# An attention and feed-forward kernel: the first k and q loads cast by GpSimd, and four later loads moved between queues

## The chip, the cores and the metric

The kernel runs on one core of one Trainium2 chip. The core has five engines that run their own instruction streams and wait for each other through semaphores: TensorE (PE: matrix products and transposes, its weight loads shown as PEld), VectorE (DVE), ScalarE (ACT), GpSimd (POOL) and SyncE (SP, which only issues DMAs here). DMAs are issued by SyncE and by GpSimd; the profile shows SyncE's as the hardware queue q1 and GpSimd's as the software queue q0, and both run on the same 16 DMA engines. The metric is device time in microseconds; less is better.

## The reference

Attention over 8 batches of 8 heads, 576 positions and 64 channels, with a causal mask and a bias that grows with the summed positive part of `s`; then a gated feed-forward block on the 4608 rows.

```python
scale = 1.0 / np.sqrt(D)
scores = scale * np.matmul(q, k.transpose(0, 1, 3, 2))
s_pos = np.maximum(s, 0.0)
cum = np.cumsum(s_pos, axis=-1)
bias = -(cum[:, :, :, None] - cum[:, :, None, :])
scores = np.where(causal, -1000000000.0, scores + np.minimum(bias, 0.0))
scores = scores - np.max(scores, axis=-1, keepdims=True)
attn = np.exp(scores)
attn = attn / (np.sum(attn, axis=-1, keepdims=True) + 1e-09)
return np.matmul(attn, v).astype(np.float32)
...
x = np.ascontiguousarray(attn_out.transpose(0, 2, 1, 3)).reshape(B * S, H * D)
...
g = x @ w_gate
silu = g * (1.0 / (1.0 + np.exp(-g)))
val = x @ w_val
return (silu * val @ w_out).astype(np.float32)
```

The inputs are float32; the kernel's products take bfloat16.

## The kernel before

The 64 heads are worked in 16 groups of four (`hb`, called batches of k and q here). For a group, k and q come in as float32 tiles `rawk`, `rawq` (`load_one`, L141), are cast to the bfloat16 tiles `ck`, `cq`, transposed, and put into the `KQ` tiles of pair `hb % 2`. Groups 0 to 4 are transposed by TensorE (`pe_transpose`, L295; `pe_transpose_half`, L306, for group 0) and copied out of the PSUM banks by `pe_out` (L319); groups 5 to 15 are written to a scratch in DRAM (`scratch`, L272) and read back with a transposing DMA (`transposes`, L281), then copied by `split` (L286). The 64 other rows of each `KQ` half carry the bias: `aug` (L183) copies rows of `HL`, which holds the summed `s` as high and low parts, into them. For the very first head the kernel does not wait for that DMA: `pick` (L910) multiplies the `HL` rows by a selecting matrix and `picked_row` (L920) writes the result.

`score_piece` (L352) makes a quarter of one head's scores (L373), ScalarE's exponential (L383) writes them to `pt`, and from head 8 on GpSimd cuts the causal triangle (L388, L393). For the first eight heads a product with `lower` (L367) does that. `av_piece` (L400) multiplies `pt` with the V tiles `VT` (L410; a column of ones gives the sums), `av_out` (L418) divides. V comes in five chunks per batch (`load_v`, L156) and is cast by `cast_v` (L167). The rows become `XT` by transposes on TensorE (`x_pe`) or by DMA.

The feed-forward block takes tiles of 512 rows: `gate_value` (L658) has 12 steps of a gate product (L643), a tanh on ScalarE (L664), a product on VectorE (L666), a value product (L643) and another product on VectorE (L677); `down_plain` (L692, tiles 0 and 1) multiplies by the output weight (L700), `down_seven` (L727) does the same in seven products per pair of halves. Weights are loaded and cast on the way by GpSimd's DMAs (`w_load`, L335): `WG`, `WV` in two column halves, `WO` in two row halves.

The order on every engine is the order of the program text (`tc.manual_schedule()`). From L949 the opening is written out by hand, heads 0 to 7 whole. Then the loop at L1059 walks the feed-forward items of each row tile; `n` counts them (a gate or a value step counts 1), and `at_item(n, f, ...)` (L1051) puts a call behind the item at which the count reaches n. Between the items, `pump` pulls attention steps of the later heads; `side` (L481) puts loads, casts and scratch steps at fixed steps of these. GpSimd casts V 1's chunks in `side` at head 11, last piece, and head 12. Group 5's k and q are cast by GpSimd at head 15 and go through the scratch.

A DMA that reuses a semaphore first waits for the earlier DMA on it: GpSimd's and SyncE's DMAs each take eight semaphores in turn. Tiles of a tag with `bufs=3`, such as `rawk` and `rawq`, are three in turn; `rawv` is one tile, so V 1 is not loaded before V 0 has been cast.

## Time and profile before

| | us |
|---|---|
| median of 3 runs | 374.07 |
| lowest, highest | 373.37, 374.59 |
| the profiled execution | 373.92 |
| its span, first to last instruction | 372.0 |

The granted TensorE clock of the span is 0.998. By stage, from a table of windows (busy us of each engine; the DMA column is the mean busy share of the 16 DMA engines, which can pass 1 where packets overlap):

| stage, us | PE | DVE | ACT | POOL | DMA |
|---|---|---|---|---|---|
| 0 to 5 | 3.56 | 3.77 | 4.02 | 4.03 | 0.55 |
| 5 to 10 | 4.11 | 4.86 | 3.92 | 4.95 | 0.91 |
| 10 to 15 | 4.31 | 4.91 | 4.27 | 4.94 | 0.98 |
| 15 to 19 | 3.45 | 3.94 | 4.00 | 3.94 | 1.06 |
| 19 to 24 | 5.00 | 3.65 | 4.62 | 4.53 | 1.05 |
| 24 to 29 | 5.00 | 3.41 | 2.97 | 4.07 | 1.27 |
| 29 to 35 | 5.22 | 5.67 | 4.99 | 1.15 | 1.23 |
| 35 to 55 | 19.85 | 15.76 | 15.05 | 11.48 | 1.20 |
| 55 to 85 | 29.75 | 18.75 | 22.30 | 20.17 | 0.93 |
| 85 to 365 | 279.60 | 223.21 | 172.96 | 153.14 | 0.61 |
| 365 to 372 | 3.34 | 3.14 | 0.82 | 0.00 | 0.42 |

Matmuls are pipelined and their ends modelled, so that a TensorE busy by this table is not TensorE at its peak. GpSimd's time includes the issuing of its DMAs, shown as DMA_DIRECT2D instructions with a duration. In the lines of a timeline or of a chain the first two columns are the start and the duration in us.

### The profile page before, as it was taken

The page shows a single profiled execution, that of the slowest core. Times are in us where ns is not written, and L with a number is a line of the kernel's source. Part 1 is how long each engine was busy: PE and PEld are TensorE (multiplying, and loading weights), DVE is VectorE, ACT ScalarE, POOL GpSimd, SP SyncE. Part 2 cuts the span into 40 slices and gives each one's busy share as a digit, 9 for nine tenths or more (in the row PEclk, how much of TensorE's full clock was granted, in tenths as well). Part 3 has the DMA queues.
Part 4 walks back from the last instruction along what each step waited for, and adds up shares of the span by engine and source line. Part 5 has one row for each costly group of instructions (what it writes and reads, how often), then busy time and mean ns, then how long its engine had stood idle before and what let it go on. Part 6 is the DMA issues. An engine that isn't in the chain of part 4 may idle for free.

```text
span 372.0 us, 8786 instructions
## 1 busy us (share of the span) xinstructions
PE 363.2 (98%) x3288; PEld 230.3 (62%) x3288; DVE 291.1 (78%) x585; ACT 239.9 (65%) x470; POOL 212.4 (57%) x325
## 2 busy tenths in 40 slices
PE   7899999999999999999999999999999999999996
PEld 6684556655555557855685558655865585476465
DVE  8978776377985899589967897699868867975984
ACT  8877776778886967688757875786565523323321
POOL 8983556955266547594749464955675516315320
PEclk9999999999999999999999999999999999999999
DMA  7999999799879996996789484994142113002003
GB/s 238 220 254 259 215 272 257 239 299 227 252 172 307 199 268 181 162 285 217 214 179 263 160 185 157 265 210 114 40 121 62 35 30 118 0 3 86 28 0 113
DMA packets 97133, 64.21 MB, mean 173 GB/s; under 512 B 77228, under 2 KB 82724, under 8 KB 97092
## 3 DMA queue, kind: packets, MB, share of 16 engines
q1 hardware_dynamic: 84964, 41.46, 46.9%
q0 software_dynamic: 12128, 22.21, 22.7%
q8 instruction: 25, 0.41, 0.5%
q14 instruction: 16, 0.13, 0.1%
HBM read 37.90 MB, written 19.86 MB: 155 GB/s over the span
## 4 chain that ended last, share of the span: by engine, by line
PE 83%; DVE 10%; DMA 2%; ACT 2%; issue 2%; POOL 1%; DVEq 0%; ACTq 0%
PE banks L643 43%; PE banks L749 17%; PE banks L373 9%; PE banks L410 7%; PE banks L700 5%; DVE kq L330 3%; DMA pk<-ks 2%; DVE pp L666 2%; DVE ht L677 1%; DVE kq L288 1%; ACT th L664 1%; POOL vt L173 1%; ACT pt L383 1%; PE banks L459 1%; PE banks L301 0%
## 5 line engine op out<-in xcount | busy, mean ns | idle before, releaser
L383 ACT ACTIVATE pt<-banks 128x512 bf16<-128x512 f32 (+1 forms) x256 | 120.4, 511 | 29.8 <-PE banks L373 17.1
L643 PE MATMUL banks<-XT,wg 128*128 128x512 bf16 x432 | 111.4, 379 | 0.4 <-DVE pp L666 0.3
L643 PE MATMUL banks<-XT,wv 128*128 128x512 bf16 x432 | 110.9, 379 | 0.1
L664 ACT ACTIVATE th<-banks 128x512 bf16<-128x512 f32 x108 | 64.7, 599 | 56.3 <-PE banks L643 51.4
L666 DVE SCALAR_TENSOR_TENSOR pp<-th,banks 128x512 bf16<-128x512 bf16 x108 | 73.7, 682 | 18.3 <-ACT th L664 18.0
L677 DVE SCALAR_TENSOR_TENSOR ht<-pp,banks 128x512 bf16<-128x512 bf16 x108 | 74.1, 687 | 10.3
L373 PE MATMUL banks<-kq 128*128 128x128 bf16 (+4 forms) x576 | 76.4, 240 | 0.8 <-DVE kq L330 0.3
L686 POOL TENSOR_TENSOR ht<-ht 128x512 bf16<-128x512 bf16 x35 | 40.4, 1154 | 53.3 <-DVE su L684 53.2
L373 PEld LDWEIGHTS <-kq 128*128 128x128 bf16 x576 | 46.1, 98 | 30.7 <-issue 2.4
L643 PEld LDWEIGHTS <-wv 128*128 128x128 bf16 x432 | 38.4, 98 | 36.2 <-issue 0.2
L643 PEld LDWEIGHTS <-wg 128*128 128x128 bf16 x432 | 38.4, 98 | 34.1 <-issue 0.7
L410 PEld LDWEIGHTS <-pt 128*128 128x128 bf16 x960 | 41.8, 98 | 17.7 <-issue 0.7
L388 POOL TENSOR_SCALAR_AFFINE_SELECT pt<-pt 128x512 bf16<-128x512 bf16 x56 | 36.6, 653 | 25.9 <-ACT pt L383 21.7
L410 PE MATMUL banks<-vt,pt 128*128 128x65 bf16 x960 | 46.8, 194 | 0.5 <-DVE ot L427 0.4
L444 POOL DMA_DIRECT2D xs<-ot x24 | 21.7, 904 | 30.4 <-DVE ot L427 28.0
L749 PEld LDWEIGHTS <-ht 128*128 128x128 bf16 x336 | 31.2, 98 | 4.3
L427 DVE TENSOR_TENSOR ot<-banks,rc 128x320 bf16<-128x320 f32 x64 | 31.5, 492 | 2.2
L188 POOL DMA_DIRECT2D kq<-HL x48 | 29.2, 610 | 0.0
L700 PE MATMUL banks<-wo,ht 128*128 128x512 bf16 x96 | 25.8, 379 | 0.0
L749 PEld LDWEIGHTS <-su 128*128 128x128 bf16 x252 | 23.6, 98 | 3.3
L814 POOL TENSOR_TENSOR ysb<-ysb 128x512 f32<-128x512 f32 x12 | 15.2, 1269 | 15.3 <-DVE ysb L808 15.3
L749 PE MATMUL banks<-WS,ht 128*128 128x256 bf16 x168 | 22.9, 273 | 0.0
(101 smaller groups left out, 377.2 us busy)
## 6 DMA issues: line engine op xcount, KB each, us to landing
out_dram<-ysb POOLq DMA_DIRECT2D x32, 256.0 KB, 4.0
rawv<-in_v_dram SPq DMA_DIRECT2D x28, 256.0 KB
rawk<-in_k_dram SPq DMA_DIRECT2D x12, 576.0 KB
rawq<-in_q_dram SPq DMA_DIRECT2D x12, 576.0 KB
xs<-ot POOLq DMA_DIRECT2D x24, 160.0 KB, 3.7
ks<-ck SPq DMA_DIRECT2D x11, 288.0 KB
qs<-cq SPq DMA_DIRECT2D x11, 288.0 KB
rawk<-in_k_dram POOLq DMA_DIRECT2D x3, 576.0 KB, 6.0
```

What stands on the lines that cost most here:

```text
L373: nc.tensor.matmul(sc[:, o : o + w], T[:, 1, e * S + 128 * tj : e * S + 128 * (tj + 1)], T[:, 0, e * S + lo : e * S + hi], start=not maske ...
L383: nc.scalar.activation(pt[:, c0 : c0 + n], sc, AF.Exp, scale=0.125)
L388: nc.gpsimd.affine_select(pt[:, 1088:1600], pt[:, 1088:1600], pattern=[[0, 4], [1, 128]], compare_op=ALU.is_ge, fill=zreg, base=0, channel ...
L410: nc.tensor.matmul(av[:, bi * (D + 1) : (bi + 1) * (D + 1)], pt[:, c0 : c0 + 128], VT[b % 2][:, tj, h, :], start=(tj == 0), stop=(tj == bi),)
L427: nc.vector.tensor_mul(ot[:, :, e * D : (e + 1) * D], av3[:, :, 0:D], rc[:, :, None].to_broadcast([128, NCH, D]),)
L643: nc.tensor.matmul(view(bs, TT), w[:, c, f0 : f0 + 128], xt[:, c, :], start=(c == 0), stop=(c == 3),)
L664: nc.scalar.activation(th, pg, AF.Tanh, scale=0.5)
L666: nc.vector.scalar_tensor_tensor(pp, in0=th, scalar=1.0, in1=pg, op0=ALU.add, op1=ALU.mult)
L677: nc.vector.scalar_tensor_tensor(hp[:, 2 * k2 : 2 * k2 + 2, :].rearrange("p a n -> p (a n)"), in0=pp, scalar=0.5, in1=pv, op0=ALU.mult, op ...
L686: (nc.vector if ft == NFT - 1 else nc.gpsimd).tensor_sub(hp[:, 1:3, :], hp[:, 1:4:2, :], hp[:, 0:3:2, :])
L700: nc.tensor.matmul(view(pys[ts_], DM), hps[ft // 2][:, 2 * (ft % 2) + half, c0 : c0 + 128], WO[j][:, ft % WKO, :], start=(ft == 0), stop=( ...
L749: nc.tensor.matmul(ps, lhs(p), rhs(p), start=(first and p == 0), stop=(last and p == NP - 1), skip_group_check=True,)
```

## The change

Six parts:

- k and q of group 0 (heads 0 to 3) are loaded by GpSimd in four half loads (`load_first`) that cast to bfloat16 on the way, into a tile ordered by pair of heads (`firsts`), instead of by SyncE in float32. The two casts on ScalarE and the two on GpSimd (`cast_half`) go. GpSimd's order at the start becomes: k and q of the first pair of heads, `ident`, k and q of the second pair, k and q of group 1, then the other memsets. The four copies of the first pair's k and q out of PSUM are all on ScalarE (the last was on VectorE).
- TensorE's warming products take a tile of zeros, `idle`, instead of `ident`, 31 instead of 32. `pick` runs the two low-part and the two high-part products of both sides in turn. The memset of `aug_rows(0, 0)` stands earlier on VectorE.
- The pad memsets cover only the k side, and those of the second pair of tiles stand behind `init_vt(0)`.
- V 0's loads on GpSimd stand ahead of group 1's q cast but for the fifth chunk, which stands behind it.
- V 1 is issued by GpSimd, a chunk each at items 5, 6, 7, 8 and 11, instead of by SyncE ahead of k and q of group 4. SyncE issues k and q of group 4 in its place, and GpSimd k and q of group 5 at item 24.
- The output weight's halves are issued at items 13 and 22 instead of 11 and 13.

```diff
+    idle = first.tile([128, 128], BF16)
...
+        def load_first(name, r):
+            if r == 0:
+                cts[name, 0] = cp.tile(
+                    [128, J, NR, D], BF16, tag="c" + name, bufs=2, name="c" + name
+                )
+                firsts[name] = cts[name, 0].rearrange("x j r d -> x (j r d)").rearrange(
+                    "x (r j d) -> x r j d", r=NR, j=J
+                )
+            nc.gpsimd.dma_start(
+                firsts[name][:, r].rearrange("x j d -> x (j d)"),
+                SRC[name][0][0, 2 * r : 2 * r + 2, :, :].rearrange(
+                    "e (p j) d -> (e p) (j d)", j=J
+                ),
+            )
...
-        for r in range(NR):
-            load_one(0, "k", (r, r + 1))
-            load_one(0, "q", (r, r + 1))
+        load_first("k", 0)
+        load_first("q", 0)
+        make_identity(nc, ident)
+        load_first("k", 1)
+        load_first("q", 1)
+        for nm in ("k", "q"):
+            load_one(1, nm, eng=nc.gpsimd)
 
         nc.vector.memset(warm, 0.0)
         nc.vector.memset(one_s, 1.0)
+        nc.vector.memset(idle, 0.0)
...
-        make_identity(nc, ident)
+        nc.vector.memset(aug_rows(0, 0)[:, :, S // 2 :], 0.0)
...
-        nc.vector.memset(aug_rows(0, 0)[:, :, S // 2 :], 0.0)
...
-                nc.gpsimd.memset(KQ[i][r][64 * r : 64 * r + 64, :, NR * S :], 0.0)
+                nc.gpsimd.memset(KQ[i][r][64 * r : 64 * r + 64, 1, NR * S :], 0.0)
...
+        pads(0)
         nc.gpsimd.memset(aug_rows(1, 0), 0.0)
-        pads(0)
-        pads(1)
-        for nm in ("k", "q"):
-            load_one(1, nm, eng=nc.gpsimd)
...
-                nc.tensor.matmul(view(b, 128), ident, ident, start=True, stop=True)
+                nc.tensor.matmul(view(b, 128), idle, idle, start=True, stop=True)
...
-        keep_warm(32, 7)
-        cast_half(0, "k", 0, nc.scalar)
-        cast_half(0, "q", 0, nc.scalar)
+        keep_warm(31, 7)
         aug(0, SP4, range(1, HB))
         aug(1, SP4)
+        load_v(0, range(4), nc.gpsimd)
         row_half("k", 0)
         row_out("k", 0, nc.scalar, nc.scalar)
-        cast_half(0, "k", 1, nc.gpsimd)
-        cast_half(0, "q", 1, nc.gpsimd)
-        load_v(0, range(5), nc.gpsimd)
         row_half("q", 0)
-        pick(1)
-        pick(0)
-        pe_out(0, "q", 0, 0, nc.scalar)
-        pe_out(0, "q", 1, 0, nc.vector)
+        row_out("q", 0, nc.scalar, nc.scalar)
+        for lo in range(2):
+            for kq in (1, 0):
+                pick(kq, lo)
...
         cast_one(1, "q", nc.gpsimd)
+        load_v(0, (4,), nc.gpsimd)
         w_load("g", 0)
         init_vt(0)
+        pads(1)
...
-        load_v(1, range(5))
         load_qk(4)
-        load_qk(5)
...
+        for c, n in enumerate((5, 6, 7, 8, 11)):
+            at_item(n, load_v, 1, (c,), nc.gpsimd)
         at_item(9, cast_one, 3, "k", nc.gpsimd)
         at_item(10, cast_one, 3, "q", nc.gpsimd)
-        at_item(11, w_load, "o", 0)
-        at_item(13, w_load, "o", 1)
+        at_item(13, w_load, "o", 0)
+        at_item(22, w_load, "o", 1)
+        for nm in ("k", "q"):
+            at_item(24, load_one, 5, nm, (0, NR), nc.gpsimd)
```

More of the change, by code (lines that the diff above doesn't have):

```diff
@@ L148, in load_one @@
                     "(r e) (p j) d -> (e p) r (j d)", e=2, j=J
+                ),
+            )
+        cts = {}
+        firsts = {}
+        def load_first(name, r):
[10 more added lines that the diff above has]
+                    "e (p j) d -> (e p) (j d)", j=J
                 ),
@@ L249 @@
         GP4 = [nc.gpsimd] * 4
-        cts = {}
         def cast_one(hb, name, eng):
@@ L256, in cast_one @@
             src_t = loaded[name, hb]
-            if eng is nc.scalar:
-                nc.scalar.copy(dst, src_t)
-            else:
-                eng.tensor_copy(dst, src_t)
-        def cast_half(hb, name, r, eng):
-            if r == 0:
-                cts[name, hb] = cp.tile([128, J, NR, D], BF16, tag="c" + name, bufs=2, name="c" + name)
-            dst = cts[name, hb][:, :, r, :]
-            src_t = loaded[name, hb][:, r, :, :]
             if eng is nc.scalar:
@@ L312, in pe_transpose_half @@
             ps = tps[name, g][0]
-            ct = cts[name, hb]
             for j in range(j0, j1):
                 nc.tensor.transpose(
-                    ps[64 * r : 64 * r + 64, j - j0, :], ct[:, j, r, :], ident
+                    ps[64 * r : 64 * r + 64, j - j0, :], firsts[name][:, r, j, :], ident
                 )
@@ L908, in row_out, with pick @@
                 pe_out(0, nm, g, r, engs[g])
-        def pick(side):
+        def pick(side, lo):
             b = PICK[side]
-            for lo in range(2):
-                for c0, c1 in ((0, 512), (512, S)):
-                    nc.tensor.matmul(
-                        banks[:, b + c0 // 512, 0 : c1 - c0], sel[:, lo, :],
-                        HL[:, lo, 1, c0:c1], start=(lo == 0), stop=(lo == 1),
-                        skip_group_check=True,
-                    )
+            for c0, c1 in ((0, 512), (512, S)):
+                nc.tensor.matmul(
+                    banks[:, b + c0 // 512, 0 : c1 - c0], sel[:, lo, :],
+                    HL[:, lo, 1, c0:c1], start=(lo == 0), stop=(lo == 1),
+                    skip_group_check=True,
+                )
         def picked_row(side):
```

## The prediction, made before the changed kernel was run

> **What bounds the kernel now.** I read the page's first part, the waits of TensorE, the chain of waits in the first 60 us, and then the queues of GpSimd and of the DMAs.
>
> ```profile
> PE 363.2 (98%) x3288; PEld 230.3 (62%) x3288; DVE 291.1 (78%) x585; ACT 239.9 (65%) x470; POOL 212.4 (57%) x325
> ```
>
> TensorE is busy for 363.2 of 372.0 us. Its waits say when it isn't:
>
> ```profile
> PE banks L900 <- POOL ident masks.py:199: 1.4, 1, 1.4
> PE banks L301 <- DVE kq L330: 0.7, 2, 0.5
> ...
> PE banks L315 <- ACT ck L268: 0.4, 1, 0.4
> ...
> PE banks L367 <- DVE kq L330: 0.3, 1, 0.3
> ```
>
> All the waits in this answer come to 4.6 us, and by the timeline 3.3 us of them lie before 19 us. Between 35 and 365 us TensorE is busy for 329.2 of 330 us. So a gain can only come from the first 19 us, or from the short stretches up to 52 us where the chain runs over other engines; any tile that is late after 19 us costs its full lateness. In the first 19 us the chain is VectorE alone, without a pause:
>
> ```profile
> 6.97 0.80 DVE HL L246
> 7.77 0.61 DVE kq L330
> 8.44 0.17 DVE kq L929
> ...
> 15.96 2.83 DVE kq L330 x4
> 18.79 0.04 issue
> 18.83 0.19 PE banks L367
> ```
>
> Beside it GpSimd is nearly as full, since it issues DMAs too:
>
> ```profile
> 4.85 0.91 POOL L145 DMA_DIRECT2D rawk<-in_k_dram  x1
> ...
> 6.54 0.92 POOL L270 CAST ck<-rawk 128x576 bf16<-128x576 f32 x1
> 7.41 0.89 POOL L270 CAST cq<-rawq 128x576 bf16<-128x576 f32 x1
> 8.25 4.41 POOL L162 DMA_DIRECT2D rawv<-in_v_dram  x5
> ...
> 17.84 0.62 POOL L173 CAST vt<-rawv 128x512 bf16<-128x512 f32 x1
> ```
>
> The third resource is the DMA engines, with a busy share of 0.9 or more in every 5 us stretch from 5 to 65 us. Later loads land where the backlog lets them: batch 3's k, issued at 22.06 us, lands 15.2 us later, and GpSimd waits for it:
>
> ```profile
> 37.35 1.14 POOL L260 CAST ck<-rawk 128x1152 bf16<-128x1152 f32 x1 [0.87 <-DMA rawk<-in_k_dram]
> ```
>
> That cast ends at 38.49; TensorE transposes its output (L301) at 38.76, with 0.27 us to spare.
>
> **The start, VectorE.** The copy of q's second group (L330 at 7.70, next instruction at 8.44) goes to ScalarE: 0.74 us off the chain. The memset of `idle` comes on: between 0.06 (a 128x1 memset, L202) and 0.17 us (64x128, L205); I take 0.10. `ident` now comes behind two issues on GpSimd, at about 0.81 + 2 x 0.62 + 0.57 = 2.6 us; VectorE, which has the L222 memset moved ahead of it, asks for it at about 3.0, so it costs nothing, and up to 0.5 if an issue costs 0.9. The picks' first halves run earlier, so L929 follows L246 at once. Sum: 0.64, less 0.1 for reserve: 0.55 us (bounds 0.1 to 0.7).
>
> **The start, ScalarE and the loads.** ScalarE loses two casts (0.67 each) and gains one copy (three take 1.97, so 0.66). The new loads are not in the trace: a 144 KB cast load into an idle machine. From below: the fastest 160 KB store lands 2.7 us after its issue; from above: GpSimd's first 576 KB load, 5.3. I take 3.7, the median of that store, the nearest in size. So k lands at 0.81 + 3.7 = 4.5, q at about 5.2; transposes take 0.5, four copies end near 7.8, L925 (0.82) near 8.6 against 8.82 now. L929 ends at 9.33 - 0.55 = 8.8 and sets the first score, so ScalarE's part is hidden by VectorE's with 0.2 us to spare. With 5.3 the spare is gone and the first score comes about 0.8 later than now.
>
> The Trainium skill, "DMA: Bandwidth & Descriptors", sections "Issuing engine by pattern" and "SWDGE vs HWDGE vs iDMA", gives simple loads to SyncE, whose first byte comes after some 0.6 us against 1 us from GpSimd, and casts to GpSimd alone. The 0.4 us between them, an estimate from that page, speaks against the change, and the sum would be the same by it, as the spare of 0.2 us and the earlier issue take it up.
>
> By the rows the difference is 0.5 us: SyncE's k load, issued at 1.45, fed its cast at 4.68, 3.2 us later, against the 3.7 taken for GpSimd.
>
> **The start, GpSimd's queue.** Added: four issues. The nearest rows are stores of 128 rows (L721, median 0.57), a 512-row load (rawv's last, 0.70) and the first load of all (0.91); I take 0.62, so 2.5 us (2.2 to 3.6). Removed: two casts, 6.54 to 8.25, 1.7 us. The four pad memsets (1.12 together) halve; I take 0.3 off (0 to 0.5). Net +0.5 us (0 to +1.9). V 0's chunk 4 issue moves past one cast, within the same queue. So chunk 3's cast ends at 18.46 + 0.5 = 18.96. Its reader, the value products L410 (30 in 1.02 us, 0.034 each), starts at 18.89 - 0.55 = 18.34 and needs chunk 3 at its tenth, 18.65: it waits. Today its 15th product waits for chunk 4's cast on VectorE (18.81 + 0.55 = 19.36); then for 18.96 + 6 x 0.034, about 19.14. The start is worth 0.2 to 0.25 us, not 0.55.
>
> **The DMA order.** V 1 leaves SyncE, whose queue now sends k, q of batch 4 right behind the `aug` rows, near 23 us. What the two kinds cost the backlog of cast weights, by the shares of the DMA queues from 28 to 36 us and from 49.5 to 53 us:
>
> ```profile
> q0 software_dynamic: 1280, 1.71, 91.1%
> q1 hardware_dynamic: 1274, 0.32, 28.8%
> ```
>
> ```profile
> q1 hardware_dynamic: 315, 0.69, 58.0%
> q0 software_dynamic: 318, 0.32, 54.3%
> ```
>
> V 1 (first fence) goes in small packets and leaves GpSimd's queue most of the time. Batch 4's plain loads (second) take turns packet by packet, and each of their packets is large. Alone (24.5 to 27 us) GpSimd's queue moves 0.46 MB in 2.5 us, 0.184 per us. With V 1, three 384 KB weight pieces land between 27.4 and 35.6 us: 8.2 us, alone 3 x 0.393 / 0.184 = 6.4, so V 1 costs 1.8, and 2.0 up to batch 3's k. Batch 4's 1.18 MB at 0.69 / 3.5 = 0.197 per us take 6.0 us, in which GpSimd's queue goes at 0.32 / 3.5 = 0.091, half its speed: 3.0 us. So batch 3's k is 1.0 later; the stream starting earlier (first issue 0.81 instead of 1.45) gives back some 0.4. It lands at 37.3 + 0.6 = 37.9 (bounds -0.4, if the new loads cost the backlog no more than V 1 did, and +1.6, if V 1 cost 1.4 and nothing is given back), its cast ends at 39.1, and TensorE, 0.25 us early, wants it at 38.5: with 0.1 for the hand-over a wait of 0.7 us (0 to 1.75). Behind the waiting cast on GpSimd stand batch 3's q cast (wanted at 42.54, now done at 39.98: free) and two selects whose readers come at 50.9. From 39.02 to 43.29 the chain runs over ScalarE and VectorE; I let that absorb 0.3.
>
> **Edits that I cost at nothing, with their cover.** V 1 issued by GpSimd waits for weight pieces to land (its semaphores are those of `wv` and `wg` loads) and holds back selects, read first at 50.9; V 1 itself lands behind the last weights (wv, today 44.2) at the 5 us that V 0's landings span, by about 50.0, and its last cast starts at 51.3 now. The second output weight is needed after eight groups of L700, at 65.7, and issued near 53 it has 12 us; the first one's trip was 10.5 in a fuller queue. Batch 4's casts no longer wait (1.66 and 1.48 us on GpSimd, off the path). k, q 5 on GpSimd near 57 must land by 64.75; such trips were 5.3 to 15.2 us, the long ones behind four weight pieces, and behind the second output weight alone I take 7. If they don't, their casts, SyncE's scratch copies and the scores at 83.3, where TensorE waits 0.26 today, move by the lateness. The first output weight has least cover: behind V 1 (50.0), 0.786 MB at 0.167 per us (0.62 MB in 4 us from 43 to 47, with V 1 beside it, is the floor) is 4.7 us, about 55, for the first L700 at 56.04 (today it lands at 50.6).
>
> **The sum.** 373.92 for the profiled execution (span 372.0 and 1.9 around it; the median of the runs, 374.07, is 0.15 above): -0.25 + 0.7 - 0.3 = +0.15 us, 374.07 on that execution. I say 374.0: no change.
>
> **The rivals.**
> 1. Batch 3's k is later still: SyncE's new loads push it by the upper bound, 1.6, and nothing is absorbed: 1.75 - 0.25, some 375.4. For it: the 315 against 318 packets, and GpSimd already waits there. Against it: the large loads might start late enough to fall behind it. It decides once that k lands after 38.8.
> 2. The first output weight is late: it lands at 57.5 instead of 55, as V 1 from GpSimd goes slower than V 0 did: +1.5, some 375.4. For it: today's spare of 5.4 us falls to 1. Against it: a TensorE delayed by rival 1 asks later. It decides once it lands after 56.0.
> 3. The whole start is kept (0.55) and batch 3's k is no later than TensorE, while the stall at 28 to 35 us shrinks too: up to -1.2, some 372.9. For it: VectorE's chain has no pause, so each tenth counts; against it: GpSimd's added issues.
> 4. GpSimd's first loads land after 5.3 us: +0.8, some 374.7. The trace shows no first load on GpSimd.
>
> **How the numbers follow.** Forecast 0.58 (own range 373.4 to 374.8), rival 1 0.14, rival 2 0.10, rival 3 0.12, rival 4 0.06. 0.3%, about what a measurement of this kernel can tell from no change, is 1.1 us. Faster by more needs nearly all of rival 3: 0.10, and 0.03 of what I don't see: 0.13. Slower: most of rivals 1 and 2, 0.20, and 0.04 of the others: 0.24. The rest, 0.63, is within. The range leaves out a tenth on each side: 372.8 to 375.7.
>
> **What would show it.** Right: the first exponential near 9.3 instead of 9.80; the value products starting near 18.3 and held by chunk 3's cast; GpSimd's wait for batch 3's k above 0.87 us, and a new TensorE wait at its L301 near 38.5 to 39. Wrong: no such wait (then the time is nearer 373.5), or a TensorE wait at the first L700, at L410 near 51 or before the first transposes. A gain of over 1.1 us would mean that TensorE's busy time hides waits that I did not count.

## The result: 1.0% slower

The changed kernel takes 378.28 us (median of 6 runs, 377.55 to 379.96), beside 373.84 for the kernel before in the same runs (6 runs, 373.37 to 377.44). The ratio is 1.0103, 95% interval 1.0072 to 1.0134. A later comparison gave 1.0095 (1.0064 to 1.0126). The profiled execution took 377.55 us with a span of 375.8, against 373.92 and 372.0: 3.8 us of span to explain.

The first part of the page, after:

```profile
PE 361.8 (96%) x3247; PEld 230.3 (61%) x3287; DVE 291.7 (78%) x585; ACT 239.8 (64%) x469; POOL 219.4 (58%) x334
```

VectorE and ScalarE work as long as before; GpSimd 7 us longer: 8.6 more for the DMAs that it now issues, 1.7 less for casts. (TensorE's busy time and count are short of some 40 records that this trace lacks.) Among the lines of TensorE's waits that the kernel before has not, these two stand behind loads and small DMAs:

```profile
PE banks L380 <- DMA kq<-HL: 2.2, 2, 1.8
...
PE banks L309 <- POOL ck L278: 0.3, 1, 0.3
```

The columns are the total, the number and the longest wait. To see where the time goes, I matched the instructions of the two traces one to one and took the difference of their starts:

| place | shift, us | what lies there |
|---|---|---|
| first exponential | +0.30 (9.80 to 10.10) | VectorE's start chain |
| 14 us | +1.40 | head 1's bias row late, L380 |
| 41 us | +1.95 | batch 3's k late, L309 |
| 46 us | +1.80 | |
| 69 us | +2.34 | bias rows of group 4 late, L380 |
| 171 us | +2.69 | VectorE and GpSimd side by side |
| 173 us to the last product | +3.23 | |
| end of span | +3.8 | the span ends 3.1 us after the last store's issue, before 2.5 |

So nothing was gained at the start, and the loss comes in small steps. The chain of waits, in its stretch from 36 to 46 us (start, duration, what), against a cast that ended at 38.49 before:

```profile
22.80 16.70 DMA rawk<-in_k_dram
39.50 0.06 issue
39.56 1.15 POOL ck L278
40.70 0.05 issue
40.75 0.45 PE banks L309 x5
```

and from 60 to 75 us, where the rows were issued at 58.29 and had landed at 62.46 before:

```profile
59.91 8.98 DMA kq<-HL
68.89 0.04 issue
68.94 0.40 PE banks L380 x4
```

The predicted place (batch 3's k) is in this list with about its predicted size. The others are not in the prediction at all.

### The profile page after: what moved, and what is told of

Its sections match the earlier page's. It is cut to its first block, busy times and chain, and to the rows that moved or that the text cites. A ratio compares the mean times of both kernels' runs of the same rounds, so it can differ in the third digit from the quotient of the medians.

```text
span 375.8 us, 8738 instructions
## 1 busy us (share of the span) xinstructions
PE 361.8 (96%) x3247; PEld 230.3 (61%) x3287; DVE 291.7 (78%) x585; ACT 239.8 (64%) x469; POOL 219.4 (58%) x334
## 4 chain that ended last, share of the span: by engine, by line
PE 73%; POOL 10%; DMA 9%; DVE 4%; issue 2%; ACT 1%; DVEq 0%; POOLq 0%; ACTq 0%
PE banks L650 39%; PE banks L756 17%; PE banks L380 8%; PE banks L417 5%; DMA rawk<-in_k_dram 4%; PE banks L707 4%; DMA kq<-HL 2%; DMA pk<-ks 2%; POOL rawv L181 1%; DVE kq L296 1%; DVE pp L673 1%; DVE ht L684 1%; POOL vt L192 1%; POOL pt L395 1%; POOL ck L278 1%
## 5 line engine op out<-in xcount | busy, mean ns | idle before, releaser
L650 PE MATMUL banks<-XT,wv 128*128 128x512 bf16 x412 | 109.3, 379 | 1.1
L380 PE MATMUL banks<-kq 128*128 128x128 bf16 (+4 forms) x576 | 76.5, 240 | 3.3 <-DMA kq<-HL 2.2
L693 POOL TENSOR_TENSOR ht<-ht 128x512 bf16<-128x512 bf16 x35 | 40.5, 1156 | 53.8 <-DVE su L691 53.7
L380 PEld LDWEIGHTS <-kq 128*128 128x128 bf16 x576 | 46.1, 98 | 33.2 <-DMA kq<-HL 2.7
L707 PE MATMUL banks<-wo,ht 128*128 128x512 bf16 x90 | 24.8, 379 | 0.3
```

The lines of the kernel that those rows point to most:

```text
L380: nc.tensor.matmul(sc[:, o : o + w], T[:, 1, e * S + 128 * tj : e * S + 128 * (tj + 1)], T[:, 0, e * S + lo : e * S + hi], start=not maske ...
L650: nc.tensor.matmul(view(bs, TT), w[:, c, f0 : f0 + 128], xt[:, c, :], start=(c == 0), stop=(c == 3),)
L693: (nc.vector if ft == NFT - 1 else nc.gpsimd).tensor_sub(hp[:, 1:3, :], hp[:, 1:4:2, :], hp[:, 0:3:2, :])
L707: nc.tensor.matmul(view(pys[ts_], DM), hps[ft // 2][:, 2 * (ft % 2) + half, c0 : c0 + 128], WO[j][:, ft % WKO, :], start=(ft == 0), stop=( ...
```

## The experiments

In every run the time is set beside runs of the kernel before on the same chip. "Shift" is against the kernel before's first profile, as in the table above. The time of one kernel scatters by 3 us and more between executions, so single profiles and medians are kept apart.

| run | what it is | us, median | ratio to before | shift at 14 us | at the end |
|---|---|---|---|---|---|
| e1 | start alone | 377.14 | 1.0048 (1.0015 to 1.0081) | +1.37 | +1.31 |
| e2 | queue moves alone | 377.95 | 1.0074 (1.0040 to 1.0109) | +1.54 | +3.12 |
| e14 | the same again | 376.04 | 1.0043 (1.0008 to 1.0079) | +0.19 | +0.42 |
| e3 | change, k, q 4 in the text at item 9 | 378.31 | 1.0084 (1.0050 to 1.0118) | +1.53 | +2.91 |
| e4 | change, k, q 5 by SyncE | 378.57 | 1.0107 (1.0054 to 1.0160) | +1.25 | +4.23 |
| e5 | kernel before again | 375.31, one run | | +0.25 | +1.39 |
| e6 | start alone, memsets first | 377.39 | 1.0057 (1.0023 to 1.0091) | +2.34 | +1.81 |
| e7 | start alone, one memset later | 380.22 | 1.0115 (1.0066 to 1.0165) | +3.75 | +6.13 |
| e8 | change, k, q 5 earlier | 377.74 | 1.0063 (1.0031 to 1.0096) | +1.41 | +2.63 |
| e9 | start alone, V 0 far behind | 378.89, one run | | +0.42 | +4.58 |
| e10 | only output weights and k, q 5 moved | 374.39 | 0.9995 (0.9962 to 1.0029) | 0.0 | +0.19 |
| e11 | before, batch 3's k ahead | 374.45 | 0.9991 (0.9960 to 1.0023) | 0.0 | -0.65 |
| e12 | queue moves, k, q 4 by GpSimd | 375.35 | 1.0025 (0.9995 to 1.0055) | 0.0 | +1.21 |
| e13 | start alone, V 0 1.5 us later | 375.34 | 1.0029 (1.0006 to 1.0052) | +0.68 | +1.08 |
| e15 | e13's start with e10's moves | 378.65 | 1.0104 (1.0069 to 1.0140) | +0.69 | +1.87 |
| e18 | the same again | 375.81, one run | | +0.69 | +1.39 |
| e16 | change again | 378.46 | 1.0095 (1.0064 to 1.0126) | +3.62 | +4.98 |
| e17 | change, V 0 1.5 us later, k, q 4 by GpSimd | 376.93 | 1.0075 (1.0049 to 1.0100) | +0.70 | +2.44 |

### Which half costs what: e1, e2, e14

e1 is the changed kernel with the second half undone, e2 the kernel before with the second half alone.

```diff
# e1, against the changed kernel
+        load_v(1, range(5))
         load_qk(4)
+        load_qk(5)
...
-        for c, n in enumerate((5, 6, 7, 8, 11)):
-            at_item(n, load_v, 1, (c,), nc.gpsimd)
...
-        at_item(13, w_load, "o", 0)
-        at_item(22, w_load, "o", 1)
-        for nm in ("k", "q"):
-            at_item(24, load_one, 5, nm, (0, NR), nc.gpsimd)
+        at_item(11, w_load, "o", 0)
+        at_item(13, w_load, "o", 1)
```

> The changed kernel's start alone: the first loads with a cast by GpSimd and all that goes with them, but V 1, k, q 4 and k, q 5 issued by SyncE in the prologue and the output weights at items 11 and 13, as in the kernel before. Theory A (each part costs its own: the start about 1.4 us by 14 us, the queue moves about 0.55 us at 40 us and 0.4 us at 69 us, an unexplained rest of 0.9 us at 169 us and 0.6 us in the tail): the first exponential at 10.1, TensorE waits for head 1's aug row near 13, batch 3's k lands within 0.5 us of 38.0, no stall at 69 us; time 375.2 to 375.9. Rival B (the start is all of it, the queue moves only pass its delay on and enlarge it): 377.5 to 378.5. Rival C (the start is made up for before the end): 373.8 to 374.4.

> The kernel before with the moves in the queues alone: V 1 issued by GpSimd at items 5, 6, 7, 8, 11, k, q 4 alone on SyncE in the prologue, output weights at items 13 and 22, k, q 5 by GpSimd at item 24; the start is as before. Theory A: batch 3's k lands near 39, 1.5 us or more later than in the kernel before (37.2), a wait of 0.3 to 0.6 us before the transposes of batch 3, aug rows of batch 4 land 8 us or more after their issue with a stall of 0.4 to 0.6 us near 68; time 374.7 to 375.4. Rival B (the queue moves cost nothing by themselves): 373.7 to 374.3.

Both halves cost by themselves. e1's profile is as theory A has it (first exponential +0.29, the wait for head 1's row, no stall at 69 us; batch 3's k at 37.32 is 0.2 us ahead of its range), but its median, 377.14, is 1.2 us above the range given; the section on the clock says why. e2 is slower than both of its theories had it, 377.95. Its profile has the wait for head 1's row (2.1 us) although the start is the old one, so the run was repeated:

> The queue moves alone once more, the same kernel as before under that name. Its first profile had a 2.1 us wait for head 1's aug row at 13.2, with a start that is the kernel before's to the letter, where four profiles (two of the kernel before, one with the output weights and k, q 5 moved, one with batch 3's k ahead) have none. Theory A (an execution's accident): no wait here, span 374 to 375, VectorE's addition near 169 at 1.84 us again. Theory B (it belongs to this program): wait of 1.5 us or more again, span 375 to 377.

Theory A: no wait this time, so with the old start this wait comes and goes. In all, one of the seven profiles with the old start has it, and all eight with the new start and V 0's first loads where the change puts them or earlier (0.9 to 3.0 us).

### The queue moves: e3, e4, e8, e10, e12

```diff
# against the changed kernel; e3: k, q 4 later in the text
-        load_qk(4)
...
+        at_item(9, load_qk, 4)
# e4: k, q 5 by SyncE
-        for nm in ("k", "q"):
-            at_item(24, load_one, 5, nm, (0, NR), nc.gpsimd)
+        at_item(12, load_qk, 5)
# e8: k, q 5 ahead of the second output weight
-            at_item(24, load_one, 5, nm, (0, NR), nc.gpsimd)
+            at_item(21, load_one, 5, nm, (0, NR), nc.gpsimd)
```

> The changed kernel with k, q of batch 4 issued by SyncE at item 9 (about 39 us) in place of the prologue (25.1 us). Theory A (the two queues take turns packet by packet, and packets of 2304 bytes take three times the turn of those of 768, so k, q 4 halve what GpSimd's queue moves from 28.7 to 34 us): batch 3's k lands near 36, 3 us or more earlier than in the changed kernel (39.5), no wait there; 0.5 us faster than the changed kernel: 377.3 to 377.9. Rival B (GpSimd's queue is late from the start, by its own backlog): it lands at 39 or later, and the time is that of the changed kernel, 378.0 to 378.6. Where the time comes down by more than 1 us, the later shifts hang on this one.

> The changed kernel with k, q of batch 5 issued by SyncE at item 12 (about 43 us) in place of GpSimd at item 24 (58 us). Theory A (batch 4's aug rows, 9 KB each, lie in GpSimd's queue behind 1.2 MB of k, q 5 and what is left of the second output weight): the aug rows land within 5 us of their issue in place of 9.0, TensorE doesn't stall near 69 us, GpSimd's cast of k 5 no longer starts late; 0.4 us faster than the changed kernel: 377.5 to 378.0. Rival B (the rows are late for another reason, the second output weight above all): landing 7 us or more after the issue, time unchanged, 378.0 to 378.6.

e3 did not do what it was meant to: SyncE has nothing else to wait for, so it issued k, q 4 at 25.08 as before, whatever item the call stands at. It is a repeat of the changed kernel, in which batch 3's k landed at 38.36 and TensorE did not wait. The same holds in e4, with an effect: k, q 5 went out at 26.12, right behind k, q 4, and doubled what SyncE's queue holds beside GpSimd's. The chain of waits of e4:

```profile
22.77 18.97 DMA rawk<-in_k_dram
41.74 0.06 issue
41.80 1.14 POOL ck L278
42.95 0.05 issue
42.99 0.45 PE banks L309 x5
```

Batch 3's k is 2.2 us later than in the changed kernel, and TensorE waits 2.6 us for the cast. With k, q 5 out of GpSimd's queue the bias rows of group 4 landed 6.5 us after their issue (theory A had 5 at most, B 7 or more), and there was no stall at 69 us, as theory A has it; the time was not A's, for the reason above. The DMA queues from 28 to 36 us, first of the changed kernel, then of e4, then of e17 (k, q 4 moved away, and V 1 not yet at its turn):

```profile
q0 software_dynamic: 1158, 1.07, 73.6%
q1 hardware_dynamic: 556, 1.19, 44.1%
```

```profile
q1 hardware_dynamic: 723, 1.57, 57.9%
q0 software_dynamic: 962, 0.72, 57.7%
```

```profile
q0 software_dynamic: 1682, 2.18, 120.5%
```

The columns are packets, MB and the share of 16 engines. What SyncE loads there, GpSimd's queue loses nearly byte for byte: 2.18 MB alone, 1.07 beside 1.19, 0.72 beside 1.57. Moved behind it (e12, e17) batch 3's k lands at 34.70 and 35.88. But one program scatters almost as much: the kernel before, profiled again, had it at 39.63 instead of 37.23,

> The kernel before, unchanged, profiled once more. In its first profile head 1's aug row is in place when TensorE asks for it (11.04); in the run with the queue moves alone, whose first 20 us are the same program, it came 2.0 us late. Theory A (the wait for this row is the kernel's own and comes and goes from one execution to the next, the change doesn't make it): the profile shows the wait of 1.5 to 2.3 us near 13 with a span of 373 to 376, or, if it doesn't, a span near 372. Theory B (the change makes the wait, the run with the queue moves alone was an exception): no wait of over 0.5 us for that row, span 371.4 to 372.5. One look can speak against B; without the wait it leaves both open.

```profile
22.32 17.31 DMA rawk<-in_k_dram
...
39.75 1.16 POOL ck L260
...
40.95 0.45 PE banks L301 x5
```

with a wait of 1.77 us before these transposes (from the end of the products ahead of them), longer than the changed kernel's. The six profiles with V 1 on GpSimd and k, q 4 alone on SyncE have this k at 37.4 to 39.6, mean 38.7; the eight with the old order of the queues up to there and V 0 where it was or 1.5 us later have it at 36.5 to 39.6, mean 37.8.

> The changed kernel with k, q 5 issued by GpSimd at item 21, ahead of the second output weight (item 22), in place of item 24, so that they use the queue from 53 to 57 us, which was idle (78 GB/s from 52 to 56). Theory A (batch 4's aug rows are late because 1.2 MB of k, q 5 lie ahead of them in the queue): the queue is empty of k, q 5 by 62 and the aug rows land within 6.5 us of their issue, no TensorE stall near 69 us; 0.4 to 1.1 us faster than the changed kernel. Theory B (whatever is issued in that stretch fills the queue up to 68 us, the second output weight in k, q 5's place): they land 8 us or more after their issue and the time is unchanged.

Theory B on the landing, A on the stall: the second output weight took k, q 5's place ahead of the bias rows, which landed 8.2 us after their issue, but at 67.06, in time; no stall at 69 us.

```diff
# e10, against the kernel before
-        load_qk(5)
...
+        at_item(13, w_load, "o", 0)
+        at_item(22, w_load, "o", 1)
+        for nm in ("k", "q"):
+            at_item(24, load_one, 5, nm, (0, NR), nc.gpsimd)
```

> The kernel before with only the output weights moved to items 13 and 22 and k, q 5 to GpSimd at item 24; V 1 stays on SyncE ahead of k, q 4. Theory A (k, q 5 ahead of batch 4's aug rows cost 0.4 to 1.1 us at 69, and the 0.8 us at 170, where GpSimd's select, store of the attention output and subtraction hold VectorE's addition up to 1.84 us, come with the V 1 move): aug rows land 8 us or more after their issue, a stall there near 69; at 170 as in the kernel before; time 0.4 to 1.1 us over before. Theory B (any of the queue moves brings the stretch at 170): VectorE's addition L685 takes 1.8 us there too, time 1.2 to 1.9 us over before.

The stall is there (rows issued at 57.38 land at 66.95, TensorE stalls 0.40 us), the stretch at 170 us is as in the kernel before, and the whole costs nothing that can be measured: 0.9995. The remaining cost of the queue moves must come with V 1 or k, q 4:

```diff
# e12, against e2
-        load_qk(4)
...
+        for nm in ("k", "q"):
+            at_item(12, load_one, 4, nm, (0, NR), nc.gpsimd)
```

> The queue moves on the kernel before's start, with k, q 4 issued by GpSimd at item 12 instead of by SyncE in the prologue, so that nothing of 2304-byte packets shares the DMA engines from 28 to 34 us; V 1 by GpSimd as in the change. Theory A (the cost of the queue moves at 172 us and after comes with V 1's issue by GpSimd): batch 3's k lands by 36.5, VectorE's addition near 169 still takes 1.84 us, the end is 0.7 us or more later than where the shift stands at 150; time 375.5 to 377. Theory B (it comes with the early k, q 4): addition 0.28 us, time 374.2 to 375.2. If head 1's aug row is late again here with the start of the kernel before, that wait is tied to V 1's move too.

1.0025, with an interval that just reaches no change; of what the queue moves cost in e2 and e14 part is gone, and no theory's time fits alone. The addition near 169 us is short here. It is long in 8 of the 9 profiles with V 1 on GpSimd and in none of the 11 with V 1 on SyncE; so it comes with V 1's move, though not always. This is what it looks like. VectorE in the kernel before, then in the changed kernel:

```profile
164.40 0.82 DVE L288 COPY kq<-pk 64x1152 bf16<-64x1152 bf16 x1
...
166.98 0.28 DVE L685 TENSOR_TENSOR su<-ht 128x256 bf16<-128x256 bf16 x1
```

```profile
166.82 0.59 DVE L296 COPY kq<-pk 64x1152 bf16<-64x1152 bf16 x1
...
169.18 1.84 DVE L692 TENSOR_TENSOR su<-ht 128x256 bf16<-128x256 bf16 x1
```

and GpSimd in the same two stretches:

```profile
164.59 0.24 POOL L393 TENSOR_SCALAR_AFFINE_SELECT pt<-pt 128x64 bf16<-128x64 bf16 x1
164.78 0.92 POOL L444 DMA_DIRECT2D xs<-ot  x1
165.72 0.65 POOL L388 TENSOR_SCALAR_AFFINE_SELECT pt<-pt 128x512 bf16<-128x512 bf16 x1
```

```profile
167.03 0.48 POOL L400 TENSOR_SCALAR_AFFINE_SELECT pt<-pt 128x64 bf16<-128x64 bf16 x1
167.93 0.93 POOL L451 DMA_DIRECT2D xs<-ot  x1 [0.42 <-issue]
168.87 0.88 POOL L395 TENSOR_SCALAR_AFFINE_SELECT pt<-pt 128x512 bf16<-128x512 bf16 x1
169.73 1.14 POOL L693 TENSOR_TENSOR ht<-ht 128x512 bf16<-128x512 bf16 x1
```

In both kernels the small select starts 0.2 us behind VectorE's copy. Before, the copy is the one that takes longer (0.82) and the select is quick; after, the copy is quick and the select takes twice its time, GpSimd's store goes out 0.7 us later relative to the rest, and the next select runs beside VectorE's addition, which takes 1.84 us instead of 0.28. The addition ends at 171.02, 0.15 us after GpSimd's subtraction (L693, to 170.87), so it looks like a wait for the neighbour's instructions to end rather than like a slower pace. TensorE is 0.8 us later from there to the end, in each of the eight. Why V 1's move tips this, 130 us later, is not shown: the select starts 0.18 to 0.21 us behind the copy in all 20 profiles, with either outcome.

### The start: e6, e7, e9, e13

VectorE's start chain by the timeline of the changed kernel:

```profile
3.90 0.78 DVE L260 TENSOR_SCALAR s_sb<-s_sb 64x576 f32<-64x576 f32 x1
4.72 1.35 DVE L261 TENSOR_TENSOR_SCAN c<-one_s,s_sb 64x576 f32<-64x576 f32 x1
6.10 0.45 DVE L264 CAST HL<-c 64x576 bf16<-64x576 f32 x1
6.59 1.07 DVE L265 TENSOR_TENSOR HL<-c,HL 64x576 bf16<-64x576 f32 x1
7.70 1.01 DVE L266 COPY HL<-HL 64x1152 bf16<-64x1152 bf16 x1
```

In the kernel before the five took 0.55, 1.35, 0.45, 0.75 and 0.80:

```profile
3.73 0.55 DVE L240 TENSOR_SCALAR s_sb<-s_sb 64x576 f32<-64x576 f32 x1
...
6.18 0.75 DVE L245 TENSOR_TENSOR HL<-c,HL 64x576 bf16<-64x576 f32 x1
6.97 0.80 DVE L246 COPY HL<-HL 64x1152 bf16<-64x1152 bf16 x1
```

GpSimd now has its DMA issues beside the first, the mask's select beside L265, and the 1.11 us memset of `kq` (L258) beside L266:

```profile
6.29 0.77 POOL L234 TENSOR_SCALAR_AFFINE_SELECT lower<-lower 128x512 bf16<-128x512 bf16 x1
...
7.29 1.11 POOL L258 MEMSET kq<- 64x1216 f32 x1
```

Before, the mask and this memset were over by 3.72. e6 and e7 move these:

```diff
# e6, against e1: k, q 1 issued behind the memsets
-        for nm in ("k", "q"):
-            load_one(1, nm, eng=nc.gpsimd)
...
         nc.gpsimd.memset(aug_rows(1, 0), 0.0)
+        for nm in ("k", "q"):
+            load_one(1, nm, eng=nc.gpsimd)
# e7, against e1: the memset behind two issues of V 0
-        nc.gpsimd.memset(aug_rows(1, 0), 0.0)
...
-        load_v(0, range(4), nc.gpsimd)
+        load_v(0, range(2), nc.gpsimd)
+        nc.gpsimd.memset(aug_rows(1, 0), 0.0)
+        load_v(0, range(2, 4), nc.gpsimd)
```

> The start alone, with k, q 1 issued behind GpSimd's mask, pads and memset instead of ahead of them, so that the memsets run from about 4.2 to 7.0 rather than from 5.7 to 8.4 beside VectorE's HL chain. Theory A (VectorE's three HL steps L264 to L266 and the step L260 are slower because GpSimd writes SBUF beside them: 0.46, 1.08, 1.01 and 0.78 us against 0.45, 0.76, 0.80 and 0.55 in the kernel before): L265 takes 0.8 to 0.95 and L266 0.80 to 0.85, HL is complete by 8.3 in place of 8.71, the first exponential at 9.6 to 9.8 in place of 10.1. Theory B (they are slower for another reason, their data or the first loads' writes): HL at 8.6 or later, first exponential at 10.0 or later. k, q 1 issued 2.8 us later land near 11.5 to 13, and the cast of k 1 waits for them. Time by A 0.3 to 0.5 us under the start alone where the aug row's wait is alike; by B the same.

> The start alone, with GpSimd's memset of batch 1's zero rows (1.11 us, 7.29 to 8.40) moved behind the second issue of V 0, so that nothing of GpSimd but DMA issues runs beside VectorE's L266. Theory A (the memset slows it): L266 takes 0.80 to 0.85 in place of 1.01, L265 stays at about 1.0 beside the select; HL complete by 8.5, first exponential at 9.9. Theory B (DMA issues slow VectorE as much, or it is something else): L266 1.0 again. The aug rows of head 1 are issued by 8.5; if they still land at 12.8 or later the wait is not made by HL's lateness.

VectorE in e6, then in e7 (whose L264 and L265 are the same steps, a line lower):

```profile
5.09 1.67 DVE L261 TENSOR_TENSOR_SCAN c<-one_s,s_sb 64x576 f32<-64x576 f32 x1
...
7.27 0.75 DVE L265 TENSOR_TENSOR HL<-c,HL 64x576 bf16<-64x576 f32 x1
8.06 0.57 DVE L266 COPY HL<-HL 64x1152 bf16<-64x1152 bf16 x1
```

```profile
6.59 1.07 DVE L264 TENSOR_TENSOR HL<-c,HL 64x576 bf16<-64x576 f32 x1
7.70 0.76 DVE L265 COPY HL<-HL 64x1152 bf16<-64x1152 bf16 x1
```

Theory A on the mechanism: the same copy takes 0.57 to 0.76 us beside DMA issues, 0.80 beside a cast (the kernel before) and 1.01 beside the memset; the subtraction 0.75 beside DMA issues and 1.07 beside the select. For L260 no run settles the neighbour: it took 0.76 in e6 too, with the mask's memset beside it, and 0.55 before with the pad memsets beside it. But e6 gained nothing: the mask and the memset now lay beside the scan, which went from 1.35 to 1.67, HL was complete at 8.63 in place of 8.71, and the first exponential came at 11.24 (at half clock, see below); A's time was wrong. In e7 the memset comes behind the bias rows of heads 4 and 5 in the program's order, so it clears them, and it has GpSimd wait for these rows, which puts the last issues of V 0 at 16 us; its time says nothing more.

e7's first two chunks of V 0 went out 1.1 us earlier, and head 1's row came later still (3.0 us of wait). That points at V 0's packets:

```diff
# e9, against e1
-        load_v(0, range(4), nc.gpsimd)
...
-        load_v(0, (4,), nc.gpsimd)
+        load_v(0, range(5), nc.gpsimd)
# e13, against e1
+        init_vt(0)
+        pads(1)
         load_v(0, range(4), nc.gpsimd)
...
         w_load("g", 0)
-        init_vt(0)
-        pads(1)
```

> The start alone, with the four issues of V 0 that stood ahead of GpSimd's cast of q 1 put behind it, so that V 0's packets of 4096 bytes (0.30 us each) are not yet in the DMA engines when head 1's aug row comes. Theory A (the row, eight packets, waits its turn between V 0's packets; with the start as before it comes a microsecond earlier, ahead of them): TensorE doesn't wait for it, or less than 0.3 us, and the shift against the kernel before at 14 us is 0.2 to 0.5 in place of 1.4. Theory B (the row is late because HL is, 0.94 us later than before, and it takes 4 us whatever else moves): the wait stays at 1.3 to 2.0. V 0, the weights and k, q 2 come 4 us later, which costs after 20 us; the whole time tells nothing.

> The start alone, with memsets that GpSimd does a few us later anyway (V tiles' ones and zeros, batch 1's pads, 1.1 to 1.4 us) put ahead of V 0's issues, so that V 0's packets reach the DMA engines about 1.3 us later, as far behind the aug rows' issue as in the kernel before. Theory A (the order of head 1's row and V 0's packets decides): wait for the row under 0.5 us, shift at 14 us 0.2 to 0.6 in place of 1.4, time 0.8 to 1.2 us under the start alone, 0.3 to 0.8 over before. Theory B (only a long delay of V 0 helps): wait over 1 us, time of the start alone.

Theory A in both, if not to the letter: e9's shift at 14 us is 0.42, but 0.6 us of wait for the row stays, and e13's 0.68 is just over its range. TensorE's waits from 9 to 16 us in e1 and in e13:

```profile
PE banks L380 <- DMA kq<-HL: 1.8, 1, 1.8
```

```profile
PE banks L309 <- DVE kq L337: 1.0, 2, 0.9
PE banks L380 <- DVE kq L935: 0.2, 1, 0.2
```

The wait for the row is gone with V 0 issued at 9.81 instead of 8.35; a wait for VectorE's copies, 0.9 us, is what stays. So HL's 0.94 us of lateness costs half as much by itself (+0.68 at 14 us in place of 1.37); the rest it costs because V 0's first packets no longer come behind the row, issued at 8.74, but ahead of it. Before, the row went out at 7.80 and V 0 at 8.25.

### The clock: e16, e17, e15, e18

> The changed kernel once more, beside the next one. Theory A (what its first profile shows is its rule): wait of 1 to 2.2 us for head 1's aug row near 13, stall of 0.4 to 1.1 at 69, VectorE's addition at 1.84 us near 169; span 375 to 376.5, ratio to the kernel before 1.006 to 1.012. Theory B (the wait for the row is a matter of the execution here as with the old start): no wait, span 374 to 374.8.

Theory A, and more: the span is 377.5, though most of the stalls have the same size as in the first profile. The table of windows (start:end, length, then busy us of each engine, granted clock, DMA share, GB/s) of e16, with its chain of waits ahead of it:

```profile
8.73 5.16 DMA kq<-HL
```

```profile
10.00:12.00 2.00, 1.25 (x16) 0.74 (x12) 1.90 (x4) 1.68 (x3) 2.00 (x3) 1.00 1.01 299
12.00:14.00 2.00, 0.07 (x2) 0.07 (x3) 1.33 (x2) 0.00 (x0) 1.48 (x3) 0.91 1.03 228
14.00:16.00 2.00, 2.00 (x15) 1.38 (x16) 0.00 (x0) 1.16 (x3) 1.94 (x4) 0.50 0.86 197
16.00:18.00 2.00, 2.00 (x24) 1.69 (x23) 1.45 (x2) 1.21 (x4) 1.84 (x6) 0.74 0.87 102
```

The row landed at 13.89, TensorE stood idle for 2.7 us, and then its granted clock was half: the three windows are short of full speed by 0.18, 1.00 and 0.52 us, 1.7 together, that is 3.4 us at half speed. Five profiles have such a stretch, all of them with the new start, and in each the same sum gives 1.7: behind a wait for the row of 3.0 and 2.7 us (e7, e16), behind the waits for a late V 0 (e9), and from 8 us on behind the transposes of q, where TensorE has about 1 us of work in 2 (e6, e8). It does not come every time: the first profile of the change, with 1.0 us of work from 6 to 8 and 1.8 us of wait for the row, has none, and neither has e2 with a wait of 2.1.

The Trainium skill, "TensorE: Matmul & The Clock Gate", Part 1, says that the clock is halved after an idle window of about 3.4 us and that the window runs freely; its section on oscillation warns of gaps above that length. The half-speed time agrees with the window; the gap that sufficed here was shorter, 2.7 us.

A run gives the mean granted clock of each execution. Of the changed kernel's 15 executions 10 are at 0.996 or below, with a median span of 377.5 against 375.5 for the other five. Of the kernel before's executions that the five comparisons count, it is 20 of 116, 374.5 against 372.3. The start alone has 5 of 12 (376.5 against 373.7), which is what lifts e1's median over its profile; the same start with V 0 1.5 us later has none in 20 in e13 and e17, though 3 of 8 in e15, which follows.

> The changed kernel with two orders mended at once: V 0's issues behind the memsets that come later anyway, and k, q 4 issued by GpSimd at item 12 instead of by SyncE in the prologue (V 1 stays on GpSimd). Theory A (the two causes add): no wait for head 1's row, batch 3's k by 36.5, addition near 169 at 0.28 us; 0.7 us from the start plus 0.4 to 1.2 from the queues over before, time 375.4 to 376.6, 2 us or so under the changed kernel. Theory B (as in the run with V 1 back on SyncE, where the parts did not add): 377.5 to 379.

e17 and e16 ran on one chip: 376.93 against 378.46. Theory A's places are as expected but for the addition near 169 us, which took 1.84 us, and its time is 0.3 us over the range. Its ten executions, none at a low clock, have a median span of 375.2, no shorter than the change's five at full clock (375.5). So in this comparison the two mended orders bought back the low clock rather than the rest, and the intervals of the two ratios overlap.

```diff
# e15 and e18 (e13 with the moves of e10), against the changed kernel
+        init_vt(0)
+        pads(1)
         load_v(0, range(4), nc.gpsimd)
...
         w_load("g", 0)
-        init_vt(0)
-        pads(1)
...
+        load_v(1, range(5))
         load_qk(4)
...
-        for c, n in enumerate((5, 6, 7, 8, 11)):
-            at_item(n, load_v, 1, (c,), nc.gpsimd)
```

> The changed kernel with V 1 put back on SyncE ahead of k, q 4, and V 0's issues behind the memsets that come later anyway. Theory A (the change's cost is two orders in the DMA queues: V 0 ahead of head 1's row, and V 1 on GpSimd with k, q 4 early): the shift at 14 us is 0.2 to 0.6, at the end 0.3 to 1.0 with a stall of about 0.4 at 69 us; time 374.7 to 375.7, 2.5 to 3.5 under the changed kernel. Theory B (the start costs more than the row's wait): 376 to 377.5. It beats the kernel before only if VectorE's start comes out ahead, which no profile has shown.

> The new start with V 0 behind the memsets, and only the output weights and k, q 5 moved, a second look: its median was 378.65 where its profile, one of its shortest executions, gives 374.4. Theory A (the times above the profile come from waits between VectorE and GpSimd that come and go, such as the 1.1 us at 119 in the first profile): a span over 375 shows stalls of 0.5 us or more that the first profile has not, at lines where VectorE and GpSimd work side by side. Theory B (from the granted clock): the same stalls, and a lower clock.

This one stays open. e15's first 70 us are close to theory A (shift 0.69 at 14 us, and not even the stall that it had at 69), but the shift at the end is 1.87 where A had 1.0 at most, and of this a stall at 119 us brings 1.1 (0.6 in e18, 0.5 in e16). There a gate product waits for rows of the attention output that come back by DMA (`XT` from `xs`), in e15 8.1 us after the issue:

```profile
119.49 0.38 PE L650 MATMUL banks<-XT,wg 128*128 128x512 bf16 x1 [0.93 <-DMA XT<-xs]
```

So this is not the wait between VectorE and GpSimd that the expectation of e18 took it for. e15's median, 378.65, is 3.3 us above that of e13, while e10's moves alone cost nothing. The low clock is not the reason either: e15's five executions above 0.996 have a median span of 376.6, e13's ten 373.3. e18 took 375.81, at full clock. The long executions of e15 (376.34 to 382.76 in all) were not traced, so what they hold is not known.

### A candidate: e11

```diff
# e11, against the kernel before
+        load_one(3, "k", eng=nc.gpsimd)
         for nm in ("g", "v"):
             w_load(nm, 1, 0)
-        load_one(3, "k", eng=nc.gpsimd)
```

> The kernel before with k of batch 3 issued by GpSimd ahead of the first halves of the second gate and value weights instead of behind them (0.79 MB). In two executions of the kernel before it landed at 37.23 and 39.63, and the second paid 1.77 us of TensorE wait for it at 40.95. Theory A (this landing decides between the faster and the slower executions of the kernel before): it lands near 31 to 33, no wait for batch 3's k, the weight halves land by 36 and 38, ahead of their first use at 40.1 and 41.7; time 0.3 to 1.0 us under before in the median, no execution with the wait. Theory B (time lost there is taken back later, or another wait takes its place): within 0.3 us of before.

The landing moved to 31.25 and there was no wait, as A has it; the time is B's, 0.9991. The profile's span is 371.3, but the kernel before also runs at 371.4 at its best. No version beat the kernel before.

## Why the prediction was wrong

The forecast was 374.0, no change; the range, 372.8 to 375.7, does not hold the result. By its steps:

- **The start, VectorE (-0.55).** This failed. The copy did leave the chain, and the multiply behind the high-part copy follows it at once (8.74), but the sum took VectorE's durations from a trace in which GpSimd's mask and memset were over by 3.72 us. The change moves these beside the chain: L260, L265 and L266 took 0.23, 0.32 and 0.21 us longer, the chain began 0.17 later (3.90 against 3.73, where 0.10 for the memset of `idle` was taken), and the first exponential came 0.30 later in place of 0.55 earlier. e6 and e7 show the mechanism for L265 and L266; the step ("the chain is VectorE alone, without a pause") had no term for a neighbour.
- **The start, ScalarE and the loads.** Right: k landed at 4.62 and q at 5.34 (predicted 4.5 and 5.2), and ScalarE's part was not what the first score waited for. The value products, put at 18.3 and held by chunk 3's cast, began at 20.28, behind that cast (over at 19.20), so this cast held nothing.
- **GpSimd's queue (+0.5).** The issues were 0.54 to 0.68 us, as taken; what was missed is what its DMAs do to others. The order of head 1's row and V 0 in the DMA engines was no step of the prediction. It cost 0.7 us (by e13) to 1.1 us in the first profile, and TensorE waited 0.9 to 3.0 us in eight. 10 of the change's 15 executions have the low clock; the one of the ten that was traced, e16, has it behind this wait.
- **The DMA order (batch 3's k at 37.9, wait 0.7).** The mechanism was right and the term was of about the right size: 39.50 in the first profile, 38.7 in the mean of six, 0.9 later than the mean of the kernels with the old order, where 0.6 was predicted; the wait 0.49. That the wait came so near to 0.7 in the first profile is partly luck: k landed 2.3 us later there than in the first profile before, past the 38.8 that rival 1 named as its sign, but TensorE asked for it 1.5 us later itself. The sign on GpSimd did not come: it waited 0.29 us for k, not above 0.87, since it was issuing V 1 until 39.27. What the prediction did not know is that one program's landing moves by 2.4 us from one execution to the next.
- **Edits costed at nothing.** V 1 (landed by 50.07), the output weights (53.57 and 64.65) and the selects made TensorE wait nowhere; the first weight landed 4.2 us ahead of its product at 57.80, where rival 2 saw 1. k, q 5 were followed to their own readers; what is issued behind them on the same queue, the bias rows of group 4, was not. It cost 0.4 us of stall at 69 us, which e10 shows to be lost in the noise of the whole. And V 1's move brings 0.8 us at 170 us, far from any load, which no step could have had from the trace of before.
- **The rivals.** Rival 1 named the right place and gave 375.4, since it had only this term. Rival 4 had the start lose, but by loads that came in time; none had it lose by its neighbours. The chance of 0.24 for slower was too low for a change whose whole gain lay in 0.55 us of one engine's chain and which reordered three queues.

The sum over the parts, in median spans of executions with a mean clock above 0.996, against the kernel before's on the same chip: the start with V 0 1.5 us later +1.4 (e13, 373.3 against 371.9), the queue moves with k, q 4 by GpSimd +1.65 (e12, 373.55 against 371.9), both +2.9 (e17, 375.2 against 372.3). So these mended halves add. The change's own halves come to more than the whole: the start +1.15 (e1, 373.7 against 372.55), the queue moves +2.3 and +3.15 (e14, 374.2 against 371.9; e2, 375.7 against 372.55). And in e15 the sum fails: +4.7 (376.6 against 371.9), with a start of +1.4 and moves of +0.3 (e10, 372.5 against 372.2). The change itself has about 3.2 (375.5 against 372.3), and the low clock in two thirds of its executions instead of a sixth, at 2 us each, makes about 1 more: together the 3.9 to 4.4 between the medians. Of these 3.2 the profile places 1.4 in VectorE's start (0.3 to 0.7) and the row (the rest), about 0.5 in batch 3's k, 0.4 to 0.6 in the bias rows, 0.8 at 170 us and up to 0.6 in the last stores; these come from single executions, and no two have the same set.

## What to carry to other kernels

A chain that sits on one engine is not costed by its own durations alone: look at what the other engine that shares its memory will now do beside it, and, where that is moved, at what it lands beside next. When a small DMA that something waits for is issued even half a microsecond later, look at which large one now gets in front of it, in the same queue or another, and follow every DMA that is issued behind a moved one, not just the moved one's readers. A wait of close to 3 us on TensorE early in a kernel can cost more than itself: here the clock fell to half for 3.4 us behind waits of 2.7 and 3.0, and not behind waits of up to 2.1, though in two profiles without such a wait; the mean granted clock of each execution shows it where a single profile does not.

## What was not expected of the hardware

- VectorE's time for one and the same instruction depends on GpSimd: a 64x1152 bfloat16 copy 0.57, 0.76, 0.80 and 1.01 us, a 128x256 addition 0.28 and 1.84, while the cast from float32 of 64x576 took 0.45 in all of them. The Trainium skill, "GPSIMD Engine Reference", section 1, says that GpSimd shares its memory interfaces with VectorE and that they collide where VectorE runs in a two-port mode or has two inputs in memory. That fits the subtraction, the scan and the addition, which have two inputs; the copy has one, and no run shows which mode it runs in. The section gives no size, which was up to six and a half times here.
- The same program lands the same load 2.4 us apart (37.23 and 39.63), with 1.77 us of TensorE wait in one and none in the other, so a profile of one execution is not the kernel.
- A bias row of 9 KB took 1.9 us at 261 us in the kernel before, where the DMA engines are busy for 0.15 of the time, and up to 9.8 us (e3, issued 59.47, landed 69.23) behind 1.2 MB on its own queue.
- A load on SyncE goes out when SyncE gets there, not at the item where its call stands in the text: 25.08 us in e3 instead of about 39.
